# A 3x3 depthwise convolution on the tensor engine: packing nine 96-row taps into seven 128-row matmuls, with on-chip copies of the input

## The chip, the cores and the metric

The kernel runs on one core of a Trainium2 chip. The metric is the time of one execution in device microseconds (us); it is about 1.8 us longer than the span from the first to the last instruction that a profile shows. The times quoted are medians over several runs, and what is read from a profile comes from one run. A program can also run in a second, slower state. Engines are named as in the profile: PE is TensorE (matmuls), PEld its weight loads, DVE is VectorE, ACT is ScalarE, POOL is GpSimd, SP the queue that issues most DMAs.

## The reference

A ConvNeXt-V2 block on one image of 512 x 512 pixels with C = 96 channels, E = 384 hidden channels, all in bf16:

```python
out = zeros_like(x)                       # 3x3 depthwise convolution, zero padding
for i in range(3):
    for j in range(3):
        out = out + xp[:, i:i+H, j:j+W, :] * dw[i, j][None, None, None, :]
h = layernorm(out)                        # over the 96 channels
h = gelu(einsum('bhwc,ce->bhwe', h, w1))
gx = sqrt((h * h).sum(axis=(1, 2)) + 1e-6)        # over the whole image
nx = gx / (gx.mean(-1) + 1e-6)
h = grn_gamma * (h * nx) + grn_beta + h
return x + einsum('bhwe,ec->bhwc', h, w2)
```

`gx` needs the whole image, so the kernel has two phases. Phase 1 computes the convolution, the norm, the first matmul, GELU and the sums of squares, and stores part of the GELU results `g` and of the normed rows `yn` to DRAM. Phase 2 loads or recomputes `g` and does the last matmul. The change touches phase 1 only.

## The kernel before

The image is handled in bands of 16 rows. One transposing DMA a band brings channels to partitions. It reads 128 elements from each pixel's start, so partitions 0 to 95 hold the pixel's own channels, and partitions 96 to 127 hold channels 0 to 31 of the next pixel, which this kernel does not use.

```python
dst = xT[:, a:a + (hi - lo), :].rearrange("p r w -> p (r w)")[:, 0:npix_t]
src = bass.AP(x_t, x_off + lo * W * C, [[C, npix_t], [1, 128]])
nc.sync.dma_start_transpose(dst, src)
```

The convolution of a row is nine matmuls that add up in PSUM, one for each tap. The weight matrix `Dc[:, t, :]` of a tap is (identity - 1/C) scaled by the tap's channel weights, so that the mean over the channels is subtracted on the way. Contraction is over 96 of 128 partitions.

```python
def stage_conv(r):
    Y = psY.tile([C, W], f32, name="Y")
    # ... taps = (0, 0) first, then the other eight (dy, dx)
    for i, (dy, dx) in enumerate(taps):
        t = (dy + 1) * 3 + (dx + 1)
        oc0, oc1 = max(0, -dx), W - max(0, dx)
        nc.tensor.matmul(Y[:, oc0:oc1], lhsT=Dc[:, t, :],
                         rhs=xT[0:C, rr + dy, oc0 + dx:oc1 + dx],
                         start=(i == 0), stop=(i == len(taps) - 1))
    # ... ACT writes y_bf = Y and ysq = Y*Y
```

Every 8 rows, 32 one-column matmuls (`S`) sum the squares, a chain of small DVE operations makes 1/sqrt(variance), and two groups of matmuls (`T`) spread it over rows. DVE copies `T` to `RT`, POOL broadcasts it over the partitions (`rbc`), and DVE multiplies (`yn`). For each pair of rows, the first matmul `U` makes three chunks of 128 hidden channels, ACT applies GELU (`gt`), DVE squares and sums (`junk`).

```python
nc.vector.tensor_tensor(out=yn[:], in0=ybfs.pop(r)[:], in1=rbcs.pop(r)[:C, :], op=ALU.mult)
# ...
nc.scalar.activation(out=gt[:], in_=U[:], func=ACTF.Gelu_apprx_tanh)
nc.vector.scalar_tensor_tensor(out=junk[:], in0=gt[:], scalar=1.0, in1=gt[:], ..., accum_out=acc[:, j, pair:pair + 1])
# ...
nc.sync.dma_start(out=g_dram[...], in_=gt[:])
# main loop: conv of row `step`, broadcast for row step-1-LAG_T, norm of row step-LAG_C, mlp two rows behind
LAG_C = 20
LAG_T = 8
```

## Time and profile before

| | before |
|---|---|
| time, median of 12 runs | 2127.88 us (2126.14 to 2129.07) |
| first convolution starts | 14.1 us |
| start of the `y_bf` evacuation of row 40 | 113.7 us |
| one row in the steady state (`y_bf` of row 40 to row 500, divided by 460) | 2.751 us |
| `y_bf` of row 511 to the first matmul of `O` in phase 2 | 73.0 us |
| first to last matmul of `O` (phase 2) | 638.2 us |

The last rows come from the start times of the instructions in the trace.

First, the table of busy times by stretches, kernel before. A line is one stretch: its bounds and its length, then the busy time and the number of instructions of PE, PEld, DVE, ACT and POOL, the granted PE clock, the busy share of the DMA engines, and GB/s.

```profile
core 0: us, PE busy (x) PEld busy (x) DVE busy (x) ACT busy (x) POOL busy (x), PEclk, DMA share, GB/s
400.00:700.00 300.00, 300.00 (x1852) 169.67 (x1849) 281.85 (x634) 262.77 (x383) 68.36 (x112) 1.00 0.55 146
```

PE is busy for all of the 300 us. DVE has 6% of room, ACT 12%. A kernel in this state should gain from less PE work, until DVE is full.

The timeline, kernel before: start, length, engine, line of the program, operation, output and inputs, count.

```profile
799.74 2.11 PE L199 MATMUL Y<-xT,Dc 96*96 96x512 bf16 x9
...
801.69 0.60 PE L288 MATMUL U<-yn,w_sb 96*128 96x512 bf16 x2
...
802.12 2.11 PE L199 MATMUL Y<-xT,Dc 96*96 96x512 bf16 x9
...
804.06 1.03 PE L288 MATMUL U<-yn,w_sb 96*128 96x512 bf16 x4
...
804.93 2.11 PE L199 MATMUL Y<-xT,Dc 96*96 96x512 bf16 x9
```

Two rows of convolution and six `U` matmuls take from 799.74 to 804.93, 5.19 us. From start to next start, a 512-column matmul takes 216 ns here (mean of the nine taps over rows 40 to 488), so nine taps are 1.944 us of the row's 2.75.

The view of one tile's instructions, kernel before, for three weight tiles (length min/median/max in ns; first and last start):

```profile
L199 PEld LDWEIGHTS <-Dc x4602: 120/123/203, 10.2 to 1407.2; 96*96 96x96 bf16 x192
...
L262 PEld LDWEIGHTS <-TS x512: 95/96/152, 51.4 to 1433.2; 128*128 128x128 bf16 x171
...
L357 PEld LDWEIGHTS <-bet_bf x3: 80/82/83, 1409.7 to 1409.7; 128*1 128x1 bf16 x3
```

A load of 96 columns lasts longer than one of 128 (123 against 96 ns). The Trainium skill ("TensorE: Matmul & The Clock Gate", Weight-path perf modes) explains it: the fast load is used only for exactly 128 weight columns. Such a load hides behind a 216 ns matmul, but not behind a one-column one.

### The profile page before, as it was taken

How to read it: one execution, taken by the hardware profiler on the slowest of the kernel's cores; microseconds unless marked ns; L12 is line 12 of the kernel's file. 1: busy time of each engine (PE TensorE's matmuls, PEld its weight loads, DVE VectorE, ACT ScalarE, POOL GpSimd, SP SyncE). 2: the span in 40 equal slices, each digit the busy share in tenths (PEclk: the TensorE clock that was granted, in tenths of full speed). 3: DMA queues.
4: the chain of work that ended last, by engine and by line, in shares of the span. 5: the costliest groups of instructions: out<-in, count | busy, mean ns of one | idle time of the engine just before them, and what ended most of it. 6: DMA issues, size and time to landing. Idle time of an engine off the chain costs nothing.

```text
span 2127.1 us, 43050 instructions
## 1 busy us (share of the span) xinstructions
PE 2008.2 (94%) x15615; PEld 1272.5 (60%) x15615; DVE 1813.7 (85%) x3617; ACT 1602.6 (75%) x2181; POOL 540.8 (25%) x903
## 2 busy tenths in 40 slices
PE   7999999999999999999999999984999999989987
PEld 4555555555555555555555555531777777777776
DVE  1799999999999999999999999996777777777776
ACT  3788888888888888888888888874555555555554
POOL 0212121221212212121221212235333333333330
PEclk9999999999999999999999999985999999999999
DMA  4654465555654456545565546326999999999994
GB/s 104 149 134 128 140 163 155 137 132 133 171 143 138 137 138 164 142 134 138 143 171 133 131 138 156 118 90 198 380 359 355 362 358 357 364 357 356 362 358 171
DMA packets 477029, 430.55 MB, mean 202 GB/s; under 512 B 321072, under 2 KB 370320, under 8 KB 476816
## 3 DMA queue, kind: packets, MB, share of 16 engines
q1 hardware_dynamic: 419472, 276.77, 46.0%
q0 software_dynamic: 30720, 125.85, 15.9%
q10 hardware_dynamic: 26624, 25.17, 4.1%
q8 instruction: 122, 2.00, 0.4%
q14 instruction: 91, 0.75, 0.1%
HBM read 176.31 MB, written 176.16 MB: 166 GB/s over the span
## 4 chain that ended last, share of the span: by engine, by line
PE 80%; DMA 8%; ACT 5%; issue 4%; POOL 2%; DVE 1%; SPq 0%; ACTq 0%; POOLq 0%; DVEq 0%
PE Y L199 47%; PE U L288 15%; PE O L415 11%; DMA xr<-in_x_dram 5%; ACT gl L398 5%; PE U L396 4%; PE S L220 2%; PE T L262 1%; DMA gl<-g_dram 1%; DVE junk L293 1%; DMA ynl<-yn_dram 1%; POOL rbc L269 1%; POOL gl L385 1%; DMA xT<-in_x_dram 1%; POOL out_dram L420 0%
## 5 line engine op out<-in xcount | busy, mean ns | idle before, releaser
L199 PE MATMUL Y<-xT,Dc 96*96 96x511 bf16 (+1 forms) x4602 | 1088.2, 380 | 14.1 <-DMA xT<-in_x_dram 14.1
L293 DVE SCALAR_TENSOR_TENSOR junk<-gt 128x1024 bf16<-128x1024 bf16 x768 | 932.5, 1232 | 89.3 <-ACT gt L291 81.4
L199 PEld LDWEIGHTS <-Dc 96*96 96x96 bf16 x4602 | 563.9, 123 | 443.6 <-DVE Dc L100 10.2
L291 ACT ACTIVATE gt<-U 128x1024 bf16<-128x1024 f32 x768 | 756.2, 1025 | 39.6 <-PE U L288 39.6
L269 POOL PARTITION_BROADCAST rbc<-RT x512 | 333.7, 773 | 1110.3 <-DVE ri L234 1039.0
L398 ACT ACTIVATE gl<-U 128x1024 bf16<-128x1024 f32 x384 | 359.0, 1041 | 278.5 <-PE U L396 166.0
L415 PEld LDWEIGHTS <-gl 128*128 128x128 bf16 x6144 | 426.3, 160 | 53.9 <-DMA gl<-g_dram 4.8
L288 PE MATMUL U<-yn,w_sb 96*128 96x512 bf16 x1536 | 429.1, 387 | 16.8 <-ACT gt L291 10.4
L207 ACT ACTIVATE y_bf<-Y 96x512 bf16<-96x512 f32 x512 | 303.3, 592 | 179.4 <-PE Y L199 179.4
L415 PE MATMUL O<-W2s,gl 128*128 128x96 bf16 x6144 | 422.1, 226 | 4.5 <-DMA gl<-g_dram 4.5
L417 DVE TENSOR_TENSOR o_sb<-O,xb 128x384 bf16<-128x384 f32 x512 | 273.2, 554 | 159.1 <-PE O L415 146.0
L209 ACT ACTIVATE ysq<-Y 96x512 bf16<-96x512 f32 x512 | 299.1, 584 | 0.0
L396 PE MATMUL U<-ynl,w_sb 96*128 96x512 bf16 x768 | 220.0, 381 | 71.6 <-ACT gl L398 53.2
L288 PEld LDWEIGHTS <-w_sb 96*128 96x128 bf16 x1536 | 148.1, 99 | 187.0 <-issue 27.5
L405 DVE TENSOR_TENSOR xb<-xr,B2bc_f 128x1536 f32<-128x1536 bf16 x128 | 224.4, 1753 | 7.5 <-issue 5.0
L274 DVE TENSOR_TENSOR yn<-y_bf,rbc 96x512 bf16<-96x512 bf16 x512 | 201.8, 413 | 1.5 <-POOL rbc L269 1.3
L385 POOL DMA_DIRECT2D gl<-g_dram x192 | 103.0, 537 | 388.8 <-PE O L415 348.1
L396 PEld LDWEIGHTS <-w_sb 96*128 96x128 bf16 x768 | 73.0, 104 | 128.2 <-issue 105.6
L265 DVE CAST RT<-T 128x512 bf16<-128x512 f32 x128 | 86.8, 678 | 0.1
L402 POOL DMA_DIRECT2D xr<-in_x_dram x128 | 69.0, 539 | 36.8 <-DVE xb L405 15.9
L220 PEld LDWEIGHTS <-ysq 96*128 96x128 bf16 x2048 | 60.7, 96 | 13.5
L220 PE MATMUL S<-ones_c,ysq 96*128 96x1 bf16 x2048 | 60.3, 163 | 0.0
(51 smaller groups left out, 419.4 us busy)
## 6 DMA issues: line engine op xcount, KB each, us to landing
g_dram<-gt SPq DMA_DIRECT2D x384, 256.0 KB, 2.6
xr<-in_x_dram POOLq DMA_DIRECT2D x128, 384.0 KB, 9.6
gl<-g_dram SPq DMA_DIRECT2D x192, 256.0 KB, 8.1
gl<-g_dram POOLq DMA_DIRECT2D x192, 256.0 KB, 6.8
yn_dram<-yn SPq DMA_DIRECT2D x256, 96.0 KB, 1.9
ynl<-yn_dram ACTq DMA_DIRECT2D x128, 192.0 KB, 9.1
out_dram<-o_sb SPq DMA_DIRECT2D x64, 384.0 KB, 7.0
out_dram<-o_sb POOLq DMA_DIRECT2D x64, 384.0 KB, 8.0
```

What stands on the lines that cost most here:

```text
L199: nc.tensor.matmul(Y[:, oc0:oc1], lhsT=Dc[:, t, :], rhs=xT[0:C, rr + dy, oc0 + dx:oc1 + dx], start=(i == 0), stop=(i == len(taps) - 1),)
L207: nc.scalar.activation(out=y_bf[:], in_=Y[:], func=ACTF.Identity)
L209: nc.scalar.activation(out=ysq[:], in_=Y[:], func=ACTF.Square)
L269: nc.gpsimd.partition_broadcast(rbc[:], RT[32 * i:32 * i + 1, :], channels=128)
L288: nc.tensor.matmul(U[:, kk, :], lhsT=w1_sb[:, j * 128:(j + 1) * 128], rhs=yy[:], start=True, stop=True)
L291: nc.scalar.activation(out=gt[:], in_=U[:], func=ACTF.Gelu_apprx_tanh)
L293: nc.vector.scalar_tensor_tensor(out=junk[:], in0=gt[:], scalar=1.0, in1=gt[:], op0=ALU.mult, op1=ALU.mult, accum_out=acc[:, j, pair:pair ...
L396: nc.tensor.matmul(U[:, i, :], lhsT=w1_sb[:, j * 128:(j + 1) * 128], rhs=ynt[:, i, :], start=True, stop=True)
L398: nc.scalar.activation(out=gts[j][:, a_:a_ + n_, :], in_=U[:], func=ACTF.Gelu_apprx_tanh)
L405: nc.vector.tensor_tensor(out=xb[:], in0=xr[:], in1=B2bc_f[:, None, :].to_broadcast([128, PXP, C]), op=ALU.add)
L415: nc.tensor.matmul(O[:, gl_, :], lhsT=lhsT, rhs=W2s[:, j, :], start=(j == 0), stop=(j == NCH - 1))
L417: nc.vector.tensor_tensor(out=o_sb[:, sub * GPS:(sub + 1) * GPS, :], in0=O[:], in1=xb[:, sub * GPS:(sub + 1) * GPS, :], op=ALU.add)
```

## The change

The intent: nine taps of 96 rows are 864 rows of contraction, which fit into seven operands of up to 128 rows.

- `SM` uses the 32 spare partitions of `xT`: tap dx = -1 on 96 partitions, and on the other 32 (the next pixel) channels 0 to 31 of tap dx = 0. Three matmuls, one for each dy.
- `SV` reads `xV`, an on-chip copy of the band with channels moved to partitions 32 to 127 and channels 64 to 95 of the previous pixel in partitions 0 to 31: tap dx = +1, and those channels of tap dx = 0. Three matmuls.
- `SR` reads `xR`, replicas of channels 32 to 63 of three neighbouring rows stacked in partitions, for what is left of tap dx = 0. One matmul.
- The shifts leave the first and the last column of a row incomplete. Six one-column matmuls (`SF`, `ST`) add what is missing.

In numbers for a row: 9 wide matmuls before, 7 wide and 6 narrow ones after. The copies are done by DMA from SBUF to SBUF: 2.36 MB a band for `xV`, 0.39 MB every 4 rows for `xR`. Besides, the lags shrink by four rows, the two halves of the broadcast move one row apart, the `g` stores move from the sync queue to POOL, and PE and ACT keep the order in which the program was written. `LAG_C` also sets the number of `y_bf` buffers (24 before, 20 after), the broadcast rows get 12 buffers instead of 14, and the first band's transpose is split in two.

```diff
-LAG_C = 20
-LAG_T = 8
+LAG_C = 16
+LAG_T = 4
...
+    def make_stacked(name, blocks):
+        st = consts.tile([128, C], bf16, name=name)
+        nc.vector.memset(st[:], 0.0)
+        for (p0, n, c0, t) in blocks:
+            tf, sel = dwsel_for(p0, n, c0)
+            nc.vector.tensor_scalar(out=st[p0:p0 + n, :], in0=sel[p0:p0 + n, :], scalar1=tf[p0:p0 + n, t:t + 1],
+                                    scalar2=None, op0=ALU.mult)
...
+            def copies(c0_, c1_):
+                nc.sync.dma_start(out=xV[32:128, c0_:c1_, :], in_=xT[0:C, c0_:c1_, :])
+                n_ = (c1_ - c0_) * W
+                nc.sync.dma_start(out=xV[0:32, c0_:c1_, :].rearrange("p r w -> p (r w)")[:, 1:n_],
+                                  in_=xT[64:C, c0_:c1_, :].rearrange("p r w -> p (r w)")[:, 0:n_ - 1])
...
+        def make_replicas(hf):            # 4 rows
+                nc.sync.dma_start(out=xR[32 * i:32 * i + 32, l_lo:l_hi, :],
+                                  in_=xT[32:64, base + rho + l_lo:base + rho + l_hi, :])
...
+            mms.append((Y[:, :], SR[0:96, :], xR[0:96, rl, :]))
+            for dy in dys:
+                mms.append((Y[:, 0:W - 1], SV[dy][:, :], xV[:, rr + dy, 1:W]))
+                mms.append((Y[:, 1:W], SM[dy][:, :], xT[:, rr + dy, 0:W - 1]))
+            for dy in dys:
+                mms.append((Y[:, W - 1:W], SF[dy][0:C, :], xT[0:C, rr + dy, W - 1:W]))
+                mms.append((Y[:, 0:1], ST[dy][0:C, :], xT[0:C, rr + dy, 0:1]))
...
-                    nc.sync.dma_start(out=g_dram[r0p // GB, j, :, r0p % GB:r0p % GB + 2, :], in_=gt[:])
+                    nc.gpsimd.dma_start(out=g_dram[r0p // GB, j, :, r0p % GB:r0p % GB + 2, :], in_=gt[:])
...
+        with tc.manual_schedule(engines={mybir.EngineType.SP}):
+            load_band(0)
+            load_band(1)
+        with tc.manual_schedule(engines={mybir.EngineType.PE, mybir.EngineType.Activation}):
...
+                    stage_bcast(rb_row // rs, 0)
+                if 0 <= rb_row - 1 < H and (rb_row - 1) % rs == rs - 1:
+                    stage_bcast((rb_row - 1) // rs, 1)
```

More of the change, by code (lines that the diff above doesn't have):

```diff
@@ L85 @@
     consts = ctx.enter_context(tc.tile_pool(name="consts", bufs=1))
-    ident_f = consts.tile([128, 128], f32, name="ident_f")
+    setup_ctx = ExitStack()
+    setup = setup_ctx.enter_context(tc.tile_pool(name="setup", bufs=1))
+    ident_f = setup.tile([128, 128], f32, name="ident_f")
     make_identity(nc, ident_f[:])
@@ L89 @@
     nc.vector.tensor_copy(out=ident_bf[:], in_=ident_f[:])
-    dw_bf = consts.tile([C, 9], bf16, name="dw_bf")
-    with nc.allow_non_contiguous_dma("tiny dw load"):
-        nc.sync.dma_start(out=dw_bf[:], in_=dw.rearrange("kh kw c -> c (kh kw)"))
-    dwc = consts.tile([C, 9], f32, name="dwc")
-    nc.vector.tensor_copy(out=dwc[:], in_=dw_bf[:])
-    IM = consts.tile([C, C], f32, name="IM")
-    nc.vector.tensor_scalar(out=IM[:], in0=ident_f[:C, :C], scalar1=-1.0 / C, scalar2=None, op0=ALU.add)
@@ L98, with dwsel_for @@
-    Dc = consts.tile([C, 9, C], bf16, name="Dc")
-    for t in range(9):
-        nc.vector.tensor_scalar(out=Dc[:, t, :], in0=IM[:], scalar1=dwc[:, t:t + 1], scalar2=None, op0=ALU.mult)
+    dw_cT = dw.rearrange("kh kw c -> c (kh kw)")
+    dwsel_cache = {}
+    def dwsel_for(p0, n, c0):
+        key = (p0, n, c0)
+        if key not in dwsel_cache:
+            tb = setup.tile([128, 9], bf16, name=f"dwsb_{p0}_{c0}")
+            with nc.allow_non_contiguous_dma("tiny dw load"):
+                nc.scalar.dma_start(out=tb[p0:p0 + n, :], in_=dw_cT[c0:c0 + n, :])
+            tf = setup.tile([128, 9], f32, name=f"dwsf_{p0}_{c0}")
+            nc.vector.tensor_copy(out=tf[p0:p0 + n, :], in_=tb[p0:p0 + n, :])
+            sel = setup.tile([128, C], f32, name=f"sel_{p0}_{c0}")
+            nc.vector.memset(sel[p0:p0 + n, :], -1.0 / C)
+            j0 = max(0, c0 - p0)
+            j1 = min(C, 128 + c0 - p0)
+            nc.vector.tensor_scalar(out=sel[p0:p0 + n, j0:j1], in0=ident_f[p0:p0 + n, j0 + p0 - c0:j1 + p0 - c0],
+                                    scalar1=-1.0 / C, scalar2=None, op0=ALU.add)
+            dwsel_cache[key] = (tf, sel)
+        return dwsel_cache[key]
@@ new lines, in make_stacked, with tap @@
+    def make_stacked(name, blocks):
[5 more added lines that the diff above has]
+                                    scalar2=None, op0=ALU.mult)
+        return st
+    def tap(dy, dx):
+        return (dy + 1) * 3 + (dx + 1)
+    CA = 32
+    assert C + CA == 128 and C - CA == 64
@@ new lines @@
+    SM = {dy: make_stacked(f"SM{dy + 1}", [(0, C, 0, tap(dy, -1)), (C, CA, 0, tap(dy, 0))]) for dy in (-1, 0, 1)}
+    SV = {dy: make_stacked(f"SV{dy + 1}", [(0, 32, 64, tap(dy, 0)), (32, 32, 0, tap(dy, 1)), (64, 64, 32, tap(dy, 1))])
+          for dy in (-1, 0, 1)}
+    SF = {dy: make_stacked(f"SF{dy + 1}", [(64, 32, 64, tap(dy, 0))]) for dy in (-1, 0, 1)}
+    SR = make_stacked("SR", [(32 * i, 32, 32, tap(i - 1, 0)) for i in range(3)])
+    ST = {dy: make_stacked(f"ST{dy + 1}", [(0, CA, 0, tap(dy, 0))]) for dy in (-1, 0, 1)}
@@ L136 @@
         xtpool = p1.enter_context(tc.tile_pool(name="xt", bufs=2))
+        xvpool = p1.enter_context(tc.tile_pool(name="xv", bufs=2))
+        xrpool1 = p1.enter_context(tc.tile_pool(name="xr1", bufs=4))
         ypool = p1.enter_context(tc.tile_pool(name="ybf", bufs=LAG_C + 4))
@@ L141 @@
         rtpool = p1.enter_context(tc.tile_pool(name="rt", bufs=3))
-        rbcpool = p1.enter_context(tc.tile_pool(name="rbc", bufs=rs + 6))
+        rbcpool = p1.enter_context(tc.tile_pool(name="rbc", bufs=rs + 4))
         ynpool = p1.enter_context(tc.tile_pool(name="yn", bufs=8))
@@ L154 @@
         xT_tiles = {}
+        xV_tiles = {}
         def load_band(b):
@@ L160, in load_band @@
             xT = xtpool.tile([128, rb + 2, W], bf16, name="xT")
+            xV = xvpool.tile([128, rb + 2, W], bf16, name="xV")
             npix = (hi - lo) * W
@@ L164, in load_band @@
             a = lo - (r0 - 1)
-            dst = xT[:, a:a + (hi - lo), :].rearrange("p r w -> p (r w)")[:, 0:npix_t]
-            src = bass.AP(x_t, x_off + lo * W * C, [[C, npix_t], [1, 128]])
-            nc.sync.dma_start_transpose(dst, src)
+            rlast = a + (hi - lo) - 1
+            cuts = [a, a + 10, a + (hi - lo)] if b == 0 else [a, a + (hi - lo)]
+            for c0_, c1_ in zip(cuts, cuts[1:]):
+                n_ = min((c1_ - a) * W, npix_t) - (c0_ - a) * W
+                dstT = xT[:, c0_:c1_, :].rearrange("p r w -> p (r w)")[:, 0:n_]
+                nc.sync.dma_start_transpose(dstT, bass.AP(x_t, x_off + (lo + c0_ - a) * W * C, [[C, n_], [1, 128]]))
@@ L168, in load_band @@
             if is_last:
                 with nc.allow_non_contiguous_dma("last 16 pixels"):
-                    nc.sync.dma_start(
-                        out=xT[0:C, a + (hi - lo) - 1, W - 16:W],
-                        in_=x[0, H - 1, W - 16:W, :].rearrange("w c -> c w"),
-                    )
+                    nc.sync.dma_start(out=xT[0:C, rlast, W - 16:W],
+                                      in_=x[0, H - 1, W - 16:W, :].rearrange("w c -> c w"))
+                    nc.sync.dma_start(out=xT[C:128, rlast, W - 16:W - 1],
+                                      in_=x[0, H - 1, W - 15:W, 0:CA].rearrange("w c -> c w"))
@@ L174, in load_band @@
             xT_tiles[b] = xT
+            xV_tiles[b] = xV
+            def copies(c0_, c1_):
[3 more added lines that the diff above has]
+                                  in_=xT[64:C, c0_:c1_, :].rearrange("p r w -> p (r w)")[:, 0:n_ - 1])
+            copies(cuts[0], cuts[1])
+            if b == 0:
+                make_replicas(0)
+                make_replicas(1)
+                copies(cuts[1], cuts[2])
@@ new lines @@
+        hb = 4 if rb % 4 == 0 else rb
+        xR_tiles = {}
+        def make_replicas(hf):
+            h0 = hf * hb
+            b = h0 // rb
+            r0 = b * rb
+            xT = xT_tiles[b]
+            base = h0 - r0 + 1
+            xR = xrpool1.tile([128, hb, W], bf16, name="xR")
+            for i in range(3):
+                rho = i - 1
+                l_lo = 1 if (h0 + rho < 0) else 0
+                l_hi = hb - 1 if (h0 + hb - 1 + rho >= H) else hb
+                if l_lo > 0:
+                    nc.vector.memset(xR[32 * i:32 * i + 32, 0:l_lo, :], 0.0)
+                if l_hi < hb:
+                    nc.vector.memset(xR[32 * i:32 * i + 32, l_hi:hb, :], 0.0)
+                nc.sync.dma_start(out=xR[32 * i:32 * i + 32, l_lo:l_hi, :],
+                                  in_=xT[32:64, base + rho + l_lo:base + rho + l_hi, :])
+            xR_tiles[hf] = xR
@@ L189, in stage_conv @@
             Y = psY.tile([C, W], f32, name="Y")
-            taps = [(0, 0)] + [
-                (dy, dx)
-                for dy in (-1, 0, 1)
-                for dx in (-1, 0, 1)
-                if (dy, dx) != (0, 0) and 0 <= r + dy < H
-            ]
-            for i, (dy, dx) in enumerate(taps):
-                t = (dy + 1) * 3 + (dx + 1)
-                oc0, oc1 = max(0, -dx), W - max(0, dx)
-                nc.tensor.matmul(
-                    Y[:, oc0:oc1],
-                    lhsT=Dc[:, t, :],
-                    rhs=xT[0:C, rr + dy, oc0 + dx:oc1 + dx],
-                    start=(i == 0),
-                    stop=(i == len(taps) - 1),
-                )
+            xV = xV_tiles[b]
+            hf = r // hb
+            xR = xR_tiles[hf]
+            rl = r - hf * hb
+            dys = [dy for dy in (0, -1, 1) if 0 <= r + dy < H]
+            mms = []
+            mms.append((Y[:, :], SR[0:96, :], xR[0:96, rl, :]))
[5 more added lines that the diff above has]
+                mms.append((Y[:, 0:1], ST[dy][0:C, :], xT[0:C, rr + dy, 0:1]))
+            for i, (o_, l_, m_) in enumerate(mms):
+                nc.tensor.matmul(o_, lhsT=l_, rhs=m_, start=(i == 0), stop=(i == len(mms) - 1))
+            if r % hb == hb - 1:
+                xR_tiles.pop(hf)
             y_bf = ypool.tile([C, W], bf16, name="y_bf")
@@ L251, in stage_chain, with stage_bcast @@
             rstds[k] = rn
-        def stage_bcast(k):
-            rstd_bf = rstds.pop(k)
-            TS = TSs[ts_counter[0] % NTS]
-            ts_counter[0] += 1
-            nc.vector.tensor_copy(out=TS[:, :, :, 0:128:32],
-                                  in_=rstd_bf[:, :].rearrange("p (s i g) -> p s g i", s=2, i=4, g=NG))
-            for st_ in range(2):
+        cur_TS = {}
+        def stage_bcast(k, st_):
+            if st_ == 0:
+                rstd_bf = rstds.pop(k)
+                cur_TS[k] = TSs[ts_counter[0] % NTS]
+                ts_counter[0] += 1
+            TS = cur_TS[k] if st_ == 0 else cur_TS.pop(k)
+            if st_ == 0:
+                nc.vector.tensor_copy(out=TS[:, :, :, 0:128:32],
+                                      in_=rstd_bf[:, :].rearrange("p (s i g) -> p s g i", s=2, i=4, g=NG))
+            if True:
                 T = psT.tile([128, W], f32, name="T")
@@ L303, in stage_mlp @@
                                       in_=gt[:, kk:kk + 1, :])
-        load_band(0)
-        total_steps = H + LAG_C + LAG_T + 5
-        for step in range(total_steps):
-            ra = step
-            if ra < H:
-                b = ra // rb
-                if ra % rb == 0 and b + 1 < nbands:
-                    load_band(b + 1)
-                stage_conv(ra)
-            rs_row = step - 1
-            if 0 <= rs_row < H and rs_row % rs == rs - 1:
-                stage_stats(rs_row // rs)
-                stage_chain(rs_row // rs)
-            rb_row = step - 1 - LAG_T
-            if 0 <= rb_row < H and rb_row % rs == rs - 1:
-                stage_bcast(rb_row // rs)
-            rc = step - LAG_C
-            if 0 <= rc < H:
-                stage_norm(rc)
-            rd = step - LAG_C - 2
-            if 0 <= rd < H and rd % 2 == 1:
-                stage_mlp(rd // 2, list(range(NCH - 1)))
-            if 0 <= rd - 1 < H and (rd - 1) % 2 == 1:
-                stage_mlp((rd - 1) // 2, [NCH - 1])
+        nhalves = H // hb
@@ new lines @@
+        with tc.manual_schedule(engines={mybir.EngineType.SP}):
+            load_band(0)
+            load_band(1)
+        with tc.manual_schedule(engines={mybir.EngineType.PE, mybir.EngineType.Activation}):
+            total_steps = H + LAG_C + LAG_T + 5
+            for step in range(total_steps):
+                ra = step
+                if ra < H:
+                    b = ra // rb
+                    if ra % hb == 0 and ra // hb + 2 < nhalves:
+                        make_replicas(ra // hb + 2)
+                    if ra % rb == 0 and 1 < b + 1 < nbands:
+                        load_band(b + 1)
+                    stage_conv(ra)
+                rs_row = step - 1
+                if 0 <= rs_row < H and rs_row % rs == rs - 1:
+                    stage_stats(rs_row // rs)
+                    stage_chain(rs_row // rs)
+                rb_row = step - 1 - LAG_T
+                if 0 <= rb_row < H and rb_row % rs == rs - 1:
+                    stage_bcast(rb_row // rs, 0)
+                if 0 <= rb_row - 1 < H and (rb_row - 1) % rs == rs - 1:
+                    stage_bcast((rb_row - 1) // rs, 1)
+                rc = step - LAG_C
+                if 0 <= rc < H:
+                    stage_norm(rc)
+                rd = step - LAG_C - 2
+                if 0 <= rd < H and rd % 2 == 1:
+                    stage_mlp(rd // 2, list(range(NCH - 1)))
+                if 0 <= rd - 1 < H and (rd - 1) % 2 == 1:
+                    stage_mlp((rd - 1) // 2, [NCH - 1])
@@ L330 @@
+    setup_ctx.close()
     with ExitStack() as pg:
```

## The prediction

> **What bounds it now.** Phase 1 (conv, norm, first matmul, GELU, squares) ends near 1460 us; phase 2, near 650 us, keeps DMA 97-100% busy at 360 GB/s (table by stretches); the change leaves its code alone. In phase 1's steady state the same table gives, per 300 us, PE busy 300.0, DVE 281, ACT 263: PE is saturated. The timeline repeats every 8 rows in 21.94 us, 2.74 us a row: nine conv taps 1.95 (217 ns each), first matmul 0.64, statistics and broadcast matmuls 0.15. DVE is busy 20.7 of these 21.94 us, a floor of 2.56-2.59 a row; ACT's is 2.41. PE binds with only 6% of room beneath it.
>
> **What the change does.** A tap contracts 96 of 128 rows. Packing 864 contraction rows into 128-row operands gives 7 full-width matmuls, plus 6 one-column edge matmuls a row.
> - Removed: 2 x 0.217 = 0.43 us PE a row.
> - Added: six edge matmuls, each with a weight load. One-column statistics matmuls take 29 ns each (32 in 0.94 us), but with 128-column weights; the Trainium skill ("TensorE: Matmul & The Clock Gate", Weight-path perf modes) says the fast load needs 128 columns; conv weights have 96. The trace agrees: loads last 82 ns (1 column), 96-99 (128 columns), 123 (96 columns), so 96 columns cost about 40 ns (estimate from these three; the page's columns/1.2 would give 80). Six exposed loads: 0.24 us (0.17-0.48).
> - Net PE: -0.19 to -0.22, to about 2.53 us a row.
> - DMA: an on-chip copy of each band (2.36 MB per 16 rows) and replicas (0.39 MB per 4 rows): about 90 GB/s on top of 142, DMA share from 0.55 to 0.8-0.9. The copies wait for the 12 us transpose; I expect them ready within the 16-row lead (41 us).
> - g stores (6 per 8 rows, about 0.54 us each as in phase 2) move to POOL, which has room. DVE's arithmetic is unchanged.
> - PE and ACT in program order: about as now.
> - Lags shorter by four rows: -5 us of fill and drain. Set-up (about 40 small DVE operations, copies before the first conv): +4 us.
>
> **Critical path.** PE's 2.53 falls under DVE's 2.56-2.59, so the bound passes to DVE, ACT at 92%: of 0.21 us saved about 0.12-0.15 shows. I expect 2.60-2.63 us a row: 512 x 0.13 = 65 us off phase 1. Phase 2 unchanged.
>
> **Prediction: 2060 us, 2010 to 2115.** Chances: faster by over 2% 0.70, within 2% 0.24, slower 0.06.
>
> **What would show each step.**
> - Conv group: about 13 matmuls a row, 7 wide; a row's conv near 1.75 us. At 1.95 or more, edge loads cost 80 ns.
> - Table by stretches: PE share of phase 1 below 98%, DVE 97% or more; chain of waits: PE waits for ACT or DVE.
> - Edge weight loads spaced about 40 ns.
> - DMA share 0.8-0.9; no long PE waits for copies, except at the start.
> - Phase 2 within 10 us of 650.
>
> **What would make it wrong.** Edge matmuls at 80 ns or more (about 2120). The sync queue waits in order for the transpose, holding yn stores: DVE stalls every 16 rows. Broadcasts on POOL slow down when DVE runs squares back to back (the drain shows eight in 19.7 us against 4.9 in steady state; the skill's "SBUF — State Buffer", Who interferes with whom, names a shared port), so a full DVE plus stores on POOL could starve norm. In the other direction, broadcasts spread over two steps may stretch DVE's small operations less: DVE's floor falls toward 2.45, and 2000 us is in reach.

## More of the kernel before

The costliest groups, kernel before: count, then busy time and the mean length of one in ns, then the idle time ahead of them.

```profile
L199 PE MATMUL Y<-xT,Dc 96*96 96x511 bf16 (+1 forms) x4602 | 1088.2, 380 | 14.1 <-DMA xT<-in_x_dram 14.1
L293 DVE SCALAR_TENSOR_TENSOR junk<-gt 128x1024 bf16<-128x1024 bf16 x768 | 932.5, 1232 | 89.3 <-ACT gt L291 81.4
L269 POOL PARTITION_BROADCAST rbc<-RT x512 | 333.7, 773 | 1110.3 <-DVE ri L234 1039.0
L274 DVE TENSOR_TENSOR yn<-y_bf,rbc 96x512 bf16<-96x512 bf16 x512 | 201.8, 413 | 1.5 <-POOL rbc L269 1.3
```

The only wait of the taps is for the first transposed band, 14.1 us. The 380 ns of one matmul overlap with the next one.

## The result, and the profile after

The kernel after takes 2087.75 us (median of 8 runs, 2086.2 to 2093.94) against 2127.88 us before: 40 us less, where 68 were forecast. The ratio is 0.9816, with a 95% interval of 0.9806 to 0.9825. A ratio here is the mean time of one kernel's fast runs over that of the other's of the same rounds, so it is not quite the ratio of the medians quoted. The gain stays just under 2%: the time lies inside the range of the prediction, but the outcome is "within 2%", to which it gave 0.24, and not "faster by over 2%", to which it gave 0.70.

Where the time went, from the start times in the two traces:

| stage | before | after | difference |
|---|---|---|---|
| up to `y_bf` of row 40 | 113.7 | 135.7 | +22.0 |
| rows 40 to 511 | 1294.3 | 1245.1 | -49.2 |
| `y_bf` of row 511 to the first `O` | 73.0 | 64.3 | -8.8 |
| first to last `O` (phase 2) | 638.2 | 635.0 | -3.2 |
| after the last `O` starts | 7.9 | 5.6 | -2.3 |
| whole span of the profiled run | 2127.1 | 2085.7 | -41.4 |

One row in the steady state takes 2.645 us, 0.106 less than before. The start gives nearly half of the saving back.

The table by stretches, kernel after, columns as before:

```profile
400.00:700.00 300.00, 293.01 (x2376) 180.72 (x2374) 288.47 (x652) 275.51 (x399) 191.52 (x200) 1.00 0.91 242
```

PE is no longer full, DVE has gone from 281.85 to 288.47 (96%, where the prediction asked for 97% or more), POOL from 68 to 192, and the DMA share from 0.55 to 0.91.

The timeline of PE, kernel after: the last wide matmul of a row, the first weight load of the edges, the six edge matmuls, and what comes next.

```profile
801.44 0.38 PE L277 MATMUL Y<-xT,SM 128*96 128x511 bf16 x1
801.44 0.12 PEld L277 LDWEIGHTS <-SF 96*96 96x96 bf16 x1
...
801.65 0.17 PE L277 MATMUL Y<-xT,SF 96*96 96x1 bf16 x1
...
801.68 0.18 PE L277 MATMUL Y<-xT,ST 96*96 96x1 bf16 x1
...
801.73 0.18 PE L277 MATMUL Y<-xT,SF 96*96 96x1 bf16 x1
...
801.77 0.18 PE L277 MATMUL Y<-xT,ST 96*96 96x1 bf16 x1
...
801.82 0.18 PE L277 MATMUL Y<-xT,SF 96*96 96x1 bf16 x1
...
801.87 0.18 PE L277 MATMUL Y<-xT,ST 96*96 96x1 bf16 x1
...
801.91 0.38 PE L341 MATMUL T<-ident_bf,TS 128*128 128x128 bf16 x4
```

The six edges run from 801.65 to 801.91, 0.26 us. Over 510 rows their mean spacing is 42 ns, and the whole convolution of this row is 1.77 us (from 800.14). Both are close to the forecast (40 ns, 1.75 us).

The waits, kernel after, between 150 and 1300 us: who waited for whom, us in total, times, longest.

```profile
PE T L341 <- DVE RT L344: 24.2, 54, 0.7
DVE yn L353 <- POOL rbc L348: 21.5, 29, 0.8
```

In this list PE waits in one place only: the second group of `T` matmuls needs the one PSUM buffer that DVE has not read yet. That is 0.056 us a row (24.2 us over 435 rows), so PE's work is at most 2.645 - 0.056 = 2.59 us a row. Added up from start to next start over rows 40 to 488, it is 2.57: seven wide taps of 216.4 ns, six edges of 42 ns, and 0.80 for `U`, `S` and `T`. No matmul waits for a copy in the steady state.

The costliest groups, kernel after:

```profile
L372 DVE SCALAR_TENSOR_TENSOR junk<-gt 128x1024 bf16<-128x1024 bf16 x768 | 942.1, 1247 | 24.5 <-ACT gt L370 24.2
...
L348 POOL PARTITION_BROADCAST rbc<-RT x512 | 680.4, 1442 | 122.7 <-DVE RT L344 120.8
...
L353 DVE TENSOR_TENSOR yn<-y_bf,rbc 96x512 bf16<-96x512 bf16 x512 | 234.7, 477 | 26.5 <-POOL rbc L348 26.4
L277 PE MATMUL Y<-xR,SR 96*96 96x512 bf16 x512 | 195.0, 381 | 36.3 <-DMA xR<-xT 36.3
```

The broadcasts on POOL last twice as long as before (773 to 1442 ns), the norm multiplies 413 to 477 ns. The last line shows the start: PE waited 36.3 us for replicas, in two waits, 25.4 us before the first row and 10.9 us before row 8.

The chain of waits in the first 60 us, kernel after (start, length, what):

```profile
15.49 8.38 DMA xV<-xT
...
24.44 14.17 DMA xT<-in_x_dram
...
40.29 11.46 DMA xR<-xT
...
51.89 3.60 PE Y L277 x13
```

and the same chain, kernel before:

```profile
3.29 10.74 DMA xT<-in_x_dram
14.08 20.29 PE Y L199 x78
```

Before, one transpose stands ahead of the convolutions. After, PE starts at 25.4 us, does eight rows, and then stands still until 51.9 us: the replicas of rows 8 to 11 sit on the sync queue behind the transpose of the second band, which occupies that queue for 12 us, and behind the copies that wait for it. The stop costs more than its length: from 51.9 to 59.5 us the granted PE clock is 0.50, and a wide matmul takes 427 ns from start to next start instead of 216.

### The profile page after: what moved, and what is told of

It is laid out like the page before. It is cut to its first block, busy times and chain, and to the rows that moved or that the text cites. A ratio compares the mean times of both kernels' runs of the same rounds, so it can differ in the third digit from the quotient of the medians.

```text
span 2085.7 us, 48029 instructions
## 1 busy us (share of the span) xinstructions
PE 1926.4 (92%) x17661; PEld 1295.5 (62%) x17661; DVE 1809.6 (87%) x3675; ACT 1611.8 (77%) x2181; POOL 1082.1 (52%) x1287
## 4 chain that ended last, share of the span: by engine, by line
PE 66%; issue 9%; DVE 8%; DMA 8%; ACT 6%; POOL 2%; SPq 1%; ACTq 0%; POOLq 0%; DVEq 0%
PE Y L277 32%; PE O L504 13%; PE U L367 12%; ACT gl L487 5%; PE U L485 5%; DVE junk L372 3%; PE S L294 2%; DVE yn L353 2%; DMA xr<-in_x_dram 2%; DMA xR<-xT 2%; DVE RT L344 2%; DMA gl<-g_dram 2%; PE T L341 1%; DMA yn_dram<-yn 1%; POOL rbc L348 1%
## 5 line engine op out<-in xcount | busy, mean ns | idle before, releaser
L372 DVE SCALAR_TENSOR_TENSOR junk<-gt 128x1024 bf16<-128x1024 bf16 x768 | 942.1, 1247 | 24.5 <-ACT gt L370 24.2
L370 ACT ACTIVATE gt<-U 128x1024 bf16<-128x1024 f32 x768 | 760.9, 1028 | 30.5 <-PE U L367 22.8
L348 POOL PARTITION_BROADCAST rbc<-RT x512 | 680.4, 1442 | 122.7 <-DVE RT L344 120.8
L277 PE MATMUL Y<-xV,SV 128*96 128x511 bf16 x1534 | 585.7, 382 | 0.0
L277 PE MATMUL Y<-xT,SM 128*96 128x511 bf16 x1534 | 583.8, 381 | 0.0
L378 POOL DMA_DIRECT2D g_dram<-gt x384 | 209.8, 549 | 417.6 <-ACT gt L370 415.2
L277 PEld LDWEIGHTS <-SM 128*96 128x96 bf16 x1534 | 190.3, 124 | 143.5 <-issue 2.0
L277 PEld LDWEIGHTS <-SV 128*96 128x96 bf16 x1534 | 189.4, 123 | 142.2 <-issue 1.3
L353 DVE TENSOR_TENSOR yn<-y_bf,rbc 96x512 bf16<-96x512 bf16 x512 | 234.7, 477 | 26.5 <-POOL rbc L348 26.4
L277 PE MATMUL Y<-xR,SR 96*96 96x512 bf16 x512 | 195.0, 381 | 36.3 <-DMA xR<-xT 36.3
L277 PEld LDWEIGHTS <-SF 96*96 96x96 bf16 x1534 | 174.0, 125 | 47.9 <-issue 0.7
L277 PEld LDWEIGHTS <-ST 96*96 96x96 bf16 x1534 | 156.5, 125 | 47.8 <-issue 0.7
```

The costliest lines, as they stand in the source:

```text
L277: nc.tensor.matmul(o_, lhsT=l_, rhs=m_, start=(i == 0), stop=(i == len(mms) - 1))
L348: nc.gpsimd.partition_broadcast(rbc[:], RT[32 * i:32 * i + 1, :], channels=128)
```

## The experiments

Two theories of the steady state. P: PE still binds, 2.59 us of work and 0.056 of waiting. D: DVE (with POOL) already binds at about 2.55 to 2.6 us and PE follows. A theory of the start, S: the copies and replicas in front of the first rows cost the 22 us. All twelve kernels were run for 3 rounds against the kernel before, whose median was between 2127.9 and 2128.6 us in each set.

### e1: conv weights padded to 128 columns

```diff
-        st = consts.tile([128, C], bf16, name=name)
+        st = consts.tile([128, 128], bf16, name=name)
-            Y = psY.tile([C, W], f32, name="Y")
+            Y = psY.tile([128, W], f32, name="Y")
```

The new columns hold zeros, and ACT reads `Y[0:C]`.

> The kernel after, with every conv stationary padded with zero columns from 96 to 128 (result stays correct). Theory P (the matmul queue still binds: of 2.645 us a row it is busy 2.59 and waits 0.056 for the broadcast matmuls): the six edge matmuls fall from 0.25 us a row to about 0.15 (25 ns each, as the 128-column statistics loads), the row falls to 2.55-2.58 us, the time to 2045-2060 us. Theory D (VectorE, with POOL, already binds and the matmul queue only follows): edges get just as short, but the row stays at 2.63-2.65 us and the time within 6 us of 2088.

Measured: 2070.98 us, ratio 0.9731 (0.9716 to 0.9745), correct; 2.610 us a row. The tile view and the timeline of e1:

```profile
L277 PEld LDWEIGHTS <-SF x1534: 95/96/151, 27.3 to 1363.2; 96*128 96x128 bf16 x192
```

```profile
802.37 0.17 PE L277 MATMUL Y<-xT,SF 96*128 96x1 bf16 x1
802.40 0.16 PE L277 MATMUL Y<-xT,ST 96*128 96x1 bf16 x1
802.43 0.16 PE L277 MATMUL Y<-xT,SF 96*128 96x1 bf16 x1
802.45 0.16 PE L277 MATMUL Y<-xT,ST 96*128 96x1 bf16 x1
```

The loads fall from 125 to 96 ns, the edges from 42 to 26 ns each, 0.10 us a row. The row falls by 0.035 only, and the waits of PE for `T` grow from 0.056 to 0.112 us a row. So neither theory holds alone: PE work was on the critical path, since less of it shortened the row, but more than half of it turned into waiting. Extra columns of zeros cost no time here (the wide matmuls stay at 216 ns) and make a narrow matmul cheaper.

### e2: no edge matmuls (wrong result)

```diff
-            for dy in dys:
-                mms.append((Y[:, W - 1:W], SF[dy][0:C, :], xT[0:C, rr + dy, W - 1:W]))
-                mms.append((Y[:, 0:1], ST[dy][0:C, :], xT[0:C, rr + dy, 0:1]))
```

> The kernel after without the six edge matmuls (wrong result on purpose at the left and right columns). It shows the floor beneath the matmul queue. Theory P: 0.25 us a row goes from TensorE (2.59 to 2.34), VectorE (busy 2.55 a row) then binds: 2.55-2.58 us a row, 2045-2058 us. Theory D: no change beyond 6 us from 2088.

Measured: 2056.36 us (2054.41 to 2065.87), ratio 0.9671 (0.9649 to 0.9694); 2.587 us a row. The table by stretches, e2:

```profile
400.00:700.00 300.00, 276.81 (x1755) 151.41 (x1754) 292.77 (x671) 279.75 (x407) 219.31 (x202) 1.00 0.96 247
```

With 0.25 us of PE work gone, the row loses 0.058. PE is down to 277 of 300 us and DVE at 293, so 2.587 us is close to DVE's floor, inside the 2.56 to 2.59 that the prediction read from the trace of before. The DMA share is 0.96 here, a rival limit; e3 reaches nearly the same row at 0.57, which speaks against it.

### e3: the kernel before with seven of nine taps (wrong result)

```diff
-                if (dy, dx) != (0, 0) and 0 <= r + dy < H
+                if (dy, dx) not in ((0, 0), (1, 0), (1, 1)) and 0 <= r + dy < H
```

> The kernel before with two of the nine taps left out (wrong result on purpose): the saving of two wide matmuls alone, without copies, replicas, edges, stores on POOL or the new order. TensorE falls from 2.75 to 2.32 us a row. If VectorE's floor in the kernel before is the 2.56-2.59 us that I read from its trace, the row comes to 2.57-2.62 us and the time to 2040-2065 us. If the time comes out near 2088, the floor is higher than read and the edges and copies of the change cost nothing; if near 2010, the floor is lower and the change's own additions took the difference.

Measured: 2032.57 us, ratio 0.9551 (0.9537 to 0.9565); 2.577 us a row, row 40 at 97.5 us. The table by stretches, e3:

```profile
400.00:700.00 300.00, 276.39 (x1762) 152.59 (x1760) 293.37 (x668) 278.80 (x409) 245.85 (x116) 1.00 0.57 156
```

It beat the expected range by 7 us, because the start is faster as well: row 40 comes 16 us earlier than in before. This is about what two taps fewer can give in this design, 95 us. The kernel after gets 40 of them. In the steady state it is 0.068 us a row short of e3, about 33 us over rows 40 to 511; at the start it is 38 us behind, and it gains 11 us between row 511 and phase 2. Note that POOL is busier here without any store on it (246 of 300 us) than before (68): between 150 and 1300 us a broadcast lasts 2244 ns instead of 734, with DVE at 98% instead of 94%.

### e4: replicas of rows 8 to 15 before the second band's transpose

```diff
             load_band(0)
+            make_replicas(2)
+            make_replicas(3)
             load_band(1)
```

> The kernel after with the replicas of rows 8 to 15 issued before the transpose of the second band, instead of behind it on the sync queue. Both theories: the 11.5 us wait of TensorE before row 8 goes; part of it may come back as a wait for the second band at row 16. 6 to 11 us less than 2088, that is 2077-2082; steady row unchanged at 2.645.

Measured: 2091.15 us, ratio 0.9823 (0.9806 to 0.9839), row 40 at 140.9 us: a miss. It is no faster than after; the 3 us between the medians lie within the spread of the runs. The timeline of the sync queue, e4:

```profile
25.02 4.72 SPq L245 DMA_DIRECT2D xR<-xT  x6
31.13 9.19 SPq L206 DMA_TRANSPOSE xT<-in_x_dram  x1
56.34 1.26 SPq L356 DMA_DIRECT2D yn_dram<-yn  x2
57.69 0.56 SPq L217 DMA_DIRECT2D xV<-xT  x1
```

The wait at row 8 is gone, but a longer one came at row 16, until 72.5 us. Two `yn` stores had been ordered ahead of the second band's copies, and the queue works in order: it stood from about 40 to 56 us for rows that were not there yet, with the copies behind them. Moving one item of an in-order queue moved the wait.

### e5: nine plain taps for the first band

Rows 0 to 15 use the taps of the kernel before, with its `Dc`; no copies and no replicas for that band.

```diff
+            if b == 0:
+                for dy in dys:
+                    for dx in (0, -1, 1):
+                        oc0, oc1 = max(0, -dx), W - max(0, dx)
+                        mms.append((Y[0:C, oc0:oc1], Dc[:, tap(dy, dx), :], xT[0:C, rr + dy, oc0 + dx:oc1 + dx]))
+                dys = []
```

> The kernel after, but rows 0 to 15 use the nine plain taps of the kernel before, so that the first band needs no copies and no replicas (result correct). Theory S (the start costs the change some 22 us because the first bands' copies and replicas stand in front of the first convolutions): row 40 comes back from 135.7 us to 113-120 us and the time falls by 15-22 us to 2066-2073, steady row unchanged at 2.645. If the loss at the start is instead set-up work on VectorE or the second band's transpose, row 40 stays above 130 and the time above 2083.

Measured: 2068.55 us (2067.15 to 2076.26), ratio 0.9728 (0.971 to 0.9746), correct; row 40 at 115.1 us, 2.645 us a row. The chain of waits in the first 60 us, e5:

```profile
5.32 7.85 DMA dwsb<-in_dw_dram
...
15.48 0.90 DVE Dc L128 x5
...
16.43 19.02 PE Y L286 x78
```

Theory S is confirmed: 20 us come back and the steady row does not move. What is left of set-up in front of the first convolution, small weight loads and DVE work, costs 2.4 us (16.4 against 14.1).

### e6: e1 with the g stores back on the sync queue

```diff
-                    nc.gpsimd.dma_start(out=g_dram[...], in_=gt[:])
+                    nc.sync.dma_start(out=g_dram[...], in_=gt[:])
```

> e1 (wide weights, 2.611 us a row, VectorE 97% busy) with the g stores put back on the sync queue. If the stores on POOL are what stretches VectorE's norm multiplies (336 ns each before, 408 now) and the broadcasts, those come back toward 340-365 ns and the row falls to 2.56-2.58: 2050-2058 us. If the stretch comes from broadcasts meeting the norm multiplies, nothing moves: 2071 within 5. If the sync queue, which also waits for the copies, holds up the stores, it gets slower than 2076.

Measured: 2105.78 us (2100.05 to 2109.25), ratio 0.9893 (0.9877 to 0.991): 35 us slower than e1. The norm multiplies stay at 427 ns from start to next start (408 in e1, 336 in before), so the stores on POOL are not needed to stretch them. The loss is the third branch of the expectation. The waits of e6 between 150 and 1300 us:

```profile
PE Y L277 <- DMA xR<-xT: 45.8, 26, 3.5
```

PE waits once a band for replicas, which have the stores ahead of them in the queue. After twelve of these waits the granted PE clock is 0.5 for 3.4 us. Of seven stretches of 64 rows from row 40 the best ran at 2.611 us a row, as in e1, the others at up to 2.758.

### e7: e1 with the second broadcast half one row later

```diff
-                if 0 <= rb_row - 1 < H and (rb_row - 1) % rs == rs - 1:
-                    stage_bcast((rb_row - 1) // rs, 1)
+                if 0 <= rb_row - 2 < H and (rb_row - 2) % rs == rs - 1:
+                    stage_bcast((rb_row - 2) // rs, 1)
```

> e1 with the second half of the broadcast matmuls one row later, so that its single PSUM buffer has been read by VectorE by then. If TensorE's wait there (0.112 us a row in e1) is a cause of its own, the row falls by 0.03-0.08 to 2.53-2.58 and the time to 2035-2057. If VectorE is the bound and this wait is only where TensorE follows it, the wait moves elsewhere and the row stays within 0.01 of 2.611, the time within 5 us of 2071.

Measured: 2092.37 us (2088.69 to 2098.25), ratio 0.9827 (0.9811 to 0.9843): slower than e1 by 21 us, which no branch expected. PE no longer waits for the PSUM buffer of `T` between 150 and 1300 us, but longer than in e1 for `TS`, which DVE writes and the same matmuls load:

```profile
PE T L341 <- DVE TS L336: 34.4, 36, 1.7
```

That is 0.080 us a row, against 0.112 for both waits in e1, and waits for replicas appeared (22.8 us of PE's weight loads). Seven stretches of 64 rows from row 40 ran at 2.608 to 2.721 us a row, against 2.611 in e1, so none gained. That the wait moved to another output of DVE speaks against the buffer as a cause of its own, but with the new waits beside it the run does not settle it.

### e8: the kernel after with the old lags

```diff
-LAG_C = 16
-LAG_T = 4
+LAG_C = 20
+LAG_T = 8
```

> The kernel after with the lags of the kernel before (20 and 8 rows instead of 16 and 4). The shorter lags were costed at 5 us of fill and drain: this should take 2090-2096 us, with the steady row unchanged at 2.645 and the drain after the last row 5-8 us longer.

Measured: 2177.93 us (2165.24 to 2193.88), ratio 1.0239 (1.0172 to 1.0305), correct. A large miss: 90 us slower than after. The verdict is "unclear", since the four runs spread from 2165 to 2194 us and the interval reaches below 2%; the profile is of the slowest of them, so its 2.860 us a row and its waits are on the high side. The waits of e8 between 150 and 1300 us:

```profile
PE Y L277 <- DMA xR<-xT: 66.3, 24, 3.9
```

The DMA issues of e8 (median us from issue to landing at the end of the line):

```profile
xT<-in_x_dram SPq DMA_TRANSPOSE x33, 20.1
```

In after the same line reads:

```profile
xT<-in_x_dram SPq DMA_TRANSPOSE x33, 13.5
```

The transposes land 7 us later, the replicas come too late once a band, and PE waits up to 3.9 us each time. The wait is not the whole price. The table by stretches, e8, just after one of these waits:

```profile
195.00:198.40 3.40, 3.40 (x15) 1.79 (x14) 2.12 (x6) 1.80 (x3) 0.00 (x0) 0.51 0.99 301
```

The granted PE clock is halved, and wide matmuls take 427 ns from start to next start. Between 150 and 1300 us this happens after 15 of the 24 waits, 72 us in all, so by estimate about 36 us of PE time are lost on top of the 66 us of waiting; in after it does not happen in that stretch. The end of phase 1 behaves as costed: from row 511 to phase 2 it takes 75.3 us against 64.3, so the short lags do give 11 us there.

### e9: the kernel before with the short lags

```diff
-LAG_C = 20
-LAG_T = 8
+LAG_C = 16
+LAG_T = 4
```

> The kernel before with the lags of the kernel after (16 and 4 rows) and nothing else. If shorter lags are worth only fill and drain, the time falls by 5-10 us to 2117-2123 and the steady row stays at 2.750. If they also help or hurt the steady state by themselves, the row moves by more than 0.01.

Measured: 2137.34 us, ratio 1.004 (1.0023 to 1.0057): 9 us slower than before. From row 511 to phase 2 it gains 10.3 us, but the row rises to 2.784 us and row 40 comes 4.0 us later. So the lags alone are no gain. They pay only together with the rest of the change. Why the row rises is not settled, but most of the stretch of the norm multiplies comes with the lags: between 150 and 1300 us they last 411 ns in before and 467 here, 478 in after and 413 in e8, with the old lags.

### e10: e8 with a third band buffer

```diff
-        xtpool = p1.enter_context(tc.tile_pool(name="xt", bufs=2))
+        xtpool = p1.enter_context(tc.tile_pool(name="xt", bufs=3))
-        junkpool = p1.enter_context(tc.tile_pool(name="junk", bufs=2))
+        junkpool = p1.enter_context(tc.tile_pool(name="junk", bufs=1))
```

> e8 (the kernel after with the old lags, 2178 us) with a third buffer for the transposed bands (and one buffer instead of two for the discarded squares, for space). Theory L: the loop of buffer release, transpose, copies and replicas takes longer than a band's 16 rows there, so TensorE waits 0.16 us a row for replicas; a third buffer lets the transpose start earlier, the wait goes and the time comes back to 2080-2105. Theory B: the DMA engines are simply full; then the wait and the time stay (above 2150).

Measured: 2120.45 us (2112.54 to 2125.59), ratio 0.9958 (0.9928 to 0.9988): 57 us of the 90 come back, between the two theories. PE's wait for replicas falls from 66.3 to 22.7 us over 150 to 1300 us. Between 400 and 700 us the DMA share is 1.00 and transposes still land after 18.5 us. The loop of buffer release, transpose and copies is the larger part. That full DMA engines are the rest is not shown: e10 moves 237 GB/s at that share, and after moves 242 at 0.91.

### e11: wide weights and a plain first band

The edits of e1 and e5 together.

> The wide weights of e1 and the plain first band of e5 together (result correct). The gains lie in different stages and should add: 2088 - 17 - 20 = 2050 us, between 2046 and 2056; steady row 2.61, row 40 near 114 us. If the tight chain of copies is disturbed by the earlier start, waits for replicas appear and the time is above 2060.

Measured: 2050.78 us (2048.76 to 2052.22), ratio 0.9633 (0.9619 to 0.9648), correct: the sum of the two, as expected, with 2.610 us a row and row 40 at 115.4 us. This version beats both kernels: 77 us under before, 37 under after.

### e12: e8 without the replicas (wrong result)

```diff
-            mms.append((Y[:, :], SR[0:96, :], xR[0:96, rl, :]))
+            mms.append((Y[:, :], SR[0:96, :], xT[0:96, rr, :]))
-                        make_replicas(ra // hb + 2)
```

> e8 (the kernel after with the old lags, 2178 us) without the replicas: the seventh wide matmul reads the transposed band itself (wrong result on purpose), same matmuls, a third less copying. Theory C (with the old lags the chain of transpose, copies and replicas comes a few us too late for each band, and that is all the loss): the once-per-band wait goes and the steady row comes to 2.65-2.70 us, the start is shorter too, 2075-2110 us in all. Theory O (the old lags give a worse order of work on VectorE and POOL by themselves): the row stays above 2.75, the time above 2130.

Measured: 2141.84 us (2139.96 to 2154.97), ratio 1.0083 (1.0049 to 1.0118); 2.780 us a row. Of the 90 us 36 come back, but 15 of these at the start (row 40 at 117.3 us, 132.5 in e8), so theory C explains about 21 us of the loss in the steady state, no more. Other waits stand where the replicas stood, over 150 to 1300 us:

```profile
DVE yn L347 <- DMA yn_dram<-yn: 33.9, 21, 4.0
ACT gt L364 <- PE U L361: 33.2, 67, 3.1
ACT gt L364 <- DMA g_dram<-gt: 28.5, 8, 5.4
```

DVE and ACT wait for buffers whose stores land late (`g` stores 8.0 us from issue, 5.0 in after), and transposes still take 18.8 us, at a DMA share of 0.85. So with the old lags the transposes and stores seem to hold each other up in some way that is not settled. No compute engine is full in e12 (PE 284 and DVE 270 of 300 us between 400 and 700), and the halved clock is there too (37.5 us in all), so the DMA side, and not the arithmetic, seems to carry the 90 us; which order of transfers makes the transposes slow stays open.

## Why the prediction was right or wrong

**Right: what bound the kernel, and the size of the edge cost.** PE was saturated, and fewer matmuls shortened the row. The edges cost 42 ns each where 40 were estimated from the lengths of three kinds of load. e1 shows the reason: with 128 columns they cost 26 ns. The estimate had some luck: 123 - 82 gives 41 ns, but the same difference for 128 columns, 96 - 82 = 14, falls short of the 26 measured.

**Right: the floor under PE.** The prediction read 2.56 to 2.59 us a row for DVE. Taking PE work away in two ways ended at 2.587 (e2) and 2.577 us (e3). The number is in part luck: it was read as busy time, and DVE's busy time a row fell from 2.58 us to 2.54 in after and 2.52 in e2 and e3; the rest of their rows is waiting. The prediction had named such a fall as a risk in the other direction.

**A little off: PE's new work.** "To about 2.53 us a row" was 2.57, and 2.59 with the gaps that the waits do not list. The prediction's own terms, 2.74 - 0.43 + 0.24, give 2.55; the edges took 0.25, and the row before was 2.751. No wait between the `T` matmuls and DVE was counted, which measures 0.056. PE therefore did not drop clear of DVE. The two run almost level and wait for each other, and the row came to 2.645 instead of 2.60 to 2.63. "The bound passes to DVE" is only half true: e1 shows that a third of further PE savings still counted. Against the middle of the forecast that is 0.03 us a row, some 14 us in all.

**The step that failed: "Set-up ... +4 us".** Up to row 40, the change lost 22 us. The prediction counted small DVE operations and the length of a few copies, not the queue they stand in. The first eight rows wait for a transpose, a copy and replicas in sequence (PE starts at 25.4 instead of 14.1 us). The next rows wait until 51.9 us for replicas issued behind the second band's transpose, and then run at half the clock until 59.5 us, which by estimate costs nearly 4 us more. e5 took copies and replicas away from the first band and got 20 us back. With the true size of this term the forecast would have been 2078, 10 us from the measured time.

**Right sign, wrong account: "lags shorter by four rows: -5 us".** The end of phase 1 gained 8.8 us, and e8 and e9 show that the lags are worth 10 to 11 us there. But they were not a small tidy-up. In the kernel before they slow the row (e9, +9 us in all). In the kernel after, going back to the old ones costs 90 us (e8), in part because the replicas then come too late and the clock is halved after each wait; the rest stays open (e10, e12). The change holds together only with them.

**Right for the kernel as it stands, but with no margin: copies ready in time, DMA share 0.8 to 0.9.** The share is 0.91, and in the steady state no matmul waits for a copy. Yet e6, e7 and e8, three small edits, each brought waits for replicas back. The prediction named stalls by the sync queue as a risk. It was right that they can happen, and in the steady state of the kernel they did not.

**Right: POOL.** It went from 541 to 1082 us busy and its broadcasts from 773 to 1442 ns, without starving the norm (21.5 us of waits between 150 and 1300 us). The Trainium skill ("SBUF — State Buffer", Who interferes with whom) says that a DVE instruction with two SBUF inputs contends with a POOL instruction that reads SBUF. The numbers agree in part: squares, norm multiplies and broadcasts are such instructions, and the broadcasts and multiplies grew longer, the squares hardly (1232 to 1247 ns). In e3, with no store on POOL and DVE at 98%, the broadcasts lengthen too; most of the multiplies' stretch came with the short lags (e9). That the shared port is the cause was not tested by itself.

**Right: phase 2.** From the first to the last `O`, 635 us against 638.

## What to carry to other kernels

When one engine is full and another is at 94%, count the gain from the work you remove only down to the second engine's floor. Read that floor from the trace before, and expect both to wait for each other a little above it. When a change feeds the engine through extra copies, cost them twice: in the steady state by the share of the DMA engines, and at the start by walking the in-order queue item by item to the first instruction that needs them; a plain path for the first block can win that back. Count a stop of PE at more than its length: in e8 the clock was halved for 3.4 or 6.8 us after most of the waits for replicas. For narrow matmuls, pad the weights to the width that loads fast, 128 columns here.

## What the Trainium skill lacked or had wrong

- "TensorE: Matmul & The Clock Gate", LDWEIGHTS (loading the stationary operand), gives columns / 1.2 ns for a load, 80 ns for 96 columns. In the traces such a load lasts 123 ns; back to back with one-column matmuls, 96-column loads came every 42 ns here, and 128-column fast loads every 26 ns (e1).
- The same page, Weight-path perf modes, says that the fast load needs 128 columns, which the runs confirm. It does not say that padding a narrower weight with zero columns is worth it: 17 us here, and the wide matmuls did not get longer (216 ns).
- "DMA: Bandwidth & Descriptors", Issuing engines are not separate DMA queues, says that issuing from several engines saves only the sequencer's time, usually small. It does not mention what else a queue decides: an item that waits holds up all behind it. Moving the stores from POOL to the sync queue cost 35 us here (e6 against e1); between 150 and 1300 us the sync queue stood 218 us waiting for ACT ahead of these stores, and PE waited 46 us for replicas.
- No page says how long a DMA transpose takes beside other traffic; "DMA: Bandwidth & Descriptors" gives its bandwidth. A band landed after 12.0 us in before (DMA share 0.55), 13.5 us in after (0.91) and 20.1 us in e8 (0.99 between 400 and 700 us).
